# Clustered attention and a SoLU layer: the first batch's clusters in one pass of products, its one-hots on 16 partitions, and a new order of all engines

## The chip, the cores and the metric

One core of a Trainium2 chip. Its engines are TensorE (PE, matmuls; PEld is its weight load), VectorE (DVE), ScalarE (ACT), GpSimd (POOL) and SyncE (SP, which here only issues DMAs). The metric is the device time of one execution in microseconds, as the median of several runs. Engines run at the same time, each in the order in which its instructions were written, and wait for each other through semaphores.

## The reference, cut to what matters

Four batches of eight heads, 768 tokens, 64 columns a head. Each query and each key is assigned to one of 16 clusters of its head (the centroid with the largest normalised product). A query attends only to keys of its own cluster. The result of all heads, 3072 tokens of 512, goes through a layer whose activation is SoLU, with a layer norm behind it.

```python
q_assign = np.argmax(np.einsum('bhsd,hcd->bhsc', q_n, c_n), axis=-1)
k_assign = np.argmax(np.einsum('bhsd,hcd->bhsc', k_n, c_n), axis=-1)
mask = q_assign[:, :, :, None] == k_assign[:, :, None, :]
scores = np.where(mask, scale * np.matmul(q, k.transpose(0, 1, 3, 2)), -1000000000.0)
attn = softmax(scores); x = attn @ v          # B, S, H*D
...
h = x @ w_in                                  # 512 -> 1024
solu = h * softmax(h)
ln = (solu - mu) / np.sqrt(var + 1e-06) * g_ln
out = ln @ w_out                              # 1024 -> 512
```

## The kernel before

**Attention.** The heads go in pairs, 16 of them (batch, pair). Of a pair, q and k are brought to a layout with the head's columns on partitions (`xt`). In the first batch TensorE does this by transposes (`tp`; L396 for the first pair, L403 for the other three) and ScalarE or VectorE copies the result out of PSUM (`xa`, `xb`; L422, L430). In later batches VectorE transposes (`xt`, L444). A cast to bf16 (`ca`, L468 to L472) writes 64 rows of a tile `qk`. Products with the normalised centroids (`cl`, L484 and L489) give a score for each token and cluster; VectorE turns them back (`tb`, L497), takes the largest (`mx`, L510), writes a one-hot (`oh`, L515) and transposes that (`ot`, L521). The one-hots are placed (`pl`, L533 to L540) in `qk` below the 64 rows. So one product of `qk` (`S`, L627) contracts over the 64 columns and over the clusters: a token pair of one cluster gets 1 more. k was scaled by 1/256, and the exponential (`E`, L635) multiplies by 32 and subtracts 32, so a pair of different clusters ends with a factor of exp(-32). No row maximum is subtracted. A head has 16 clusters, and two heads' one-hots come out on 32 partitions; the even head contracts over 80 rows, the odd head over 96, where a memset (`bl`, L549) blanks the 16 rows of the other head in k.

**Three pairs with two tokens in a row.** In the first batch, tokens lie 6 to a partition in DRAM order. Pairs 1 to 3 (`twelve` in the code) load both heads in one DMA and their transposes yield, on the 128 partitions, two neighbouring tokens' columns of one head. So their centroid products, in the kernel before, run in two passes: for each of four groups, one pass for each head, with a table of centroids (`c_by_two`, written by `cf`, L913) that is zero outside the pass's own head; the two add up in PSUM.

**Values and normalisation.** Values (`V`, L654) are products of the exponentials with v and a column of ones; `N` (L666, L679) divides by that column. One PSUM tile holds a group's values, so a group's first value product waits until the group before is normalised.

**SoLU layer.** The 24 units of 128 tokens each take: the transposed x (the first by TensorE, `ptx` L719, and a copy `tx` L725; the others by DMA, L709), eight products with `w_in` (`h`, L744, 128x512 each, two a token of the order), the negated maximum (`hm`, L750), the exponential (`ex`, L756), `u`, the product of the two (L763), the statistics (`bn`, `ag`), a factor (`at`, `al` on GpSimd), u transposed (`tu`, mostly by DMA), eight products with `w_out` (`y`, L813), and the scaling (`sc`, L830 on ScalarE, L832 on VectorE) with the output DMA. The products with `w_in` share three banks of PSUM (`hreg`): the second unit's second half writes a bank that the first unit's `u` reads. `w_out` is centred once (`su` L595 and L598, `me` L604, `ce` L607), its bf16 form is `w_out_c`, whose place holds tables of the first pairs until then. `w_in` is loaded by four DMAs (`li`) and cast by GpSimd (`wi`, L578).

**What sets the order.** Every piece of work is added to a class, `Weave`, with a name (kind and numbers), an engine, what it needs, and an estimated cost. `ORDER` gives for each engine a text of kinds with counts; `AWAY` names the pieces that another engine than the usual one does. `Weave.run` writes the instructions out in this order. The costs serve to interleave the engines' queues at writing; the order within an engine is that of the text. `fl` is two and `wm` 25 `idle` matmuls (L859), which nothing reads.

**The stages.** Until about 45 us there is only attention (loads, transposes, clusters, scores, exponentials, values of the first batch); from the first product with `w_in` at 45.13 us both parts run interleaved; the SoLU layer's last unit ends the kernel.

## Time and profile before

| what | value |
| --- | --- |
| median of 3 runs | 223.9 us (223.2, 223.9, 224.44) |
| span of the profiled execution | 222.4 us |
| TensorE busy | 214.8 us in 2518 instructions |
| VectorE busy | 199.1 us in 363 |
| ScalarE busy | 194.7 us in 382 |
| GpSimd busy | 126.6 us in 252 |
| exponentials of attention, ScalarE | 276, 143.2 us |
| scores, TensorE | 600, 87.4 us |
| values, TensorE | 1152 |
| products with `w_in` (177 of 192 recorded) and `w_out` (169 of 200) | 48.3 and 45.1 us |

The span is that of one profiled execution; the page has no other time for it, so the runs' median, 1.5 us longer, is the time to set it against. A row of groups reads: line, engine, operation, out<-in, partitions x elements, count | busy time, mean of one in ns | idle time of the engine before them and what ended it. A row of the timeline begins with the time in us at which a run of like instructions starts and the time that the run covers. "PEclk" is the TensorE clock that the throttle granted, 1.00 being full. The span is not the sum of anything: an engine's busy time counts only where the others wait for it.

### The profile page before, as it was taken

The numbers are of one execution on the slowest core, as the hardware profiler recorded it, in microseconds if no ns is written. First come the engines' busy times: TensorE is split into PE (matmuls) and PEld (weight loads), VectorE is DVE, ScalarE is ACT, GpSimd is POOL, SyncE is SP. The second block draws the span as 40 slices with busy tenths as digits, with TensorE's granted clock in tenths as the row PEclk, the third lists the DMA queues.
The fourth block names the chain that finished last, engine by engine and source line by source line (L and its number), as shares of the span: only waits on it lengthen the run. The fifth ranks groups of instructions, "written<-read, shape, count | busy, mean of one in ns | idle before, by whom it ended". The sixth has DMA issues, their size and how long they took to land.

```text
span 222.4 us, 6852 instructions
## 1 busy us (share of the span) xinstructions
PE 214.8 (97%) x2518; PEld 151.8 (68%) x2548; DVE 199.1 (90%) x363; ACT 194.7 (88%) x382; POOL 126.6 (57%) x252
## 2 busy tenths in 40 slices
PE   8999899999999999999999999999999999999993
PEld 7765577767777687777777666676767767665452
DVE  2789999999999999899989999999999979999891
ACT  3899999999999999999999989999999989795352
POOL 3189597759884986188837674783746101226131
PEclk9999999999999999999999999999999999999999
DMA  6998989797799979899999897998922928565623
GB/s 157 352 388 221 193 165 284 203 172 165 127 175 237 180 141 215 136 193 166 153 211 239 156 185 150 151 168 158 230 99 50 115 78 145 117 165 121 166 98 143
DMA packets 122433, 38.74 MB, mean 174 GB/s; under 512 B 111448, under 2 KB 117152, under 8 KB 122400
## 3 DMA queue, kind: packets, MB, share of 16 engines
q1 hardware_dynamic: 121680, 37.82, 79.8%
q10 hardware_dynamic: 720, 0.49, 0.7%
q8 instruction: 20, 0.33, 0.7%
q14 instruction: 13, 0.11, 0.1%
HBM read 23.11 MB, written 6.29 MB: 132 GB/s over the span
## 4 chain that ended last, share of the span: by engine, by line
PE 91%; DVE 3%; issue 2%; ACT 2%; DVEq 0%; ACTq 0%
PE sps L627 27%; PE hreg L744 18%; PE yps L813 17%; PE ops L654 16%; PE csc L489 4%; PE hreg L627 2%; PE idle_p L859 2%; PE csc L484 1%; PE hreg L403 1%; PE hreg L396 1%; ACT qk L468 1%; PE hreg L813 1%; ACT e L635 1%; DVE u L763 1%; DVE w_sum L598 1%
## 5 line engine op out<-in xcount | busy, mean ns | idle before, releaser
L635 ACT ACTIVATE e<-sps 128x512 bf16<-128x512 f32 (+1 forms) x276 | 143.2, 609 | 10.2 <-PE sps L627 9.8
L627 PE MATMUL sps<-qk 96*128 96x256 bf16 (+5 forms) x600 | 87.4, 263 | 0.7 <-ACT e L635 0.4
L627 PEld LDWEIGHTS <-qk 96*128 96x128 bf16 (+1 forms) x636 | 59.6, 121 | 24.5 <-issue 8.8
L654 PEld LDWEIGHTS <-e 128*128 128x128 bf16 x1152 | 49.9, 97 | 9.3 <-issue 1.9
L654 PE MATMUL ops<-v,e 128*128 128x65 bf16 x1152 | 54.3, 193 | 0.4 <-DVE x L679 0.4
L744 PE MATMUL hreg<-w_in_sb,xT 128*128 128x512 bf16 x177 | 48.3, 378 | 0.8
L813 PE MATMUL yps<-w_out_c,uT 128*128 128x512 bf16 x169 | 45.1, 379 | 0.8
L540 POOL COPY qk<-oht 32x384 f32<-32x384 f32 (+1 forms) x49 | 24.2, 494 | 21.5 <-DVE oht L521 15.7
L763 DVE TENSOR_TENSOR u<-e_sb,hreg 128x1024 bf16<-128x1024 bf16 (+1 forms) x25 | 29.1, 1169 | 2.7 <-ACT e_sb L756 2.1
L774 DVE BATCH_NORM_STATS2 bs<-u 128x6 f32<-128x512 bf16 x48 | 31.3, 677 | 0.0
L750 DVE TENSOR_REDUCE nmax<-hreg 128x1 f32<-128x1024 f32 x24 | 29.1, 1213 | 2.0 <-PE hreg L744 1.7
L756 ACT ACTIVATE e_sb<-hreg,nmax 128x1024 bf16<-128x1024 f32 x24 | 26.9, 1121 | 4.5 <-DVE nmax L750 4.4
L790 POOL TENSOR_SCALAR esq<-es,mv 128x1 f32<-128x1 f32 x24 | 8.3, 344 | 33.6 <-DVE mv L778 30.3
L813 PEld LDWEIGHTS <-uT 128*128 128x128 bf16 x200 | 18.0, 97 | 13.1 <-issue 0.3
L744 PEld LDWEIGHTS <-xT 128*128 128x128 bf16 x192 | 17.6, 97 | 11.3 <-ACT e L635 0.3
L472 POOL TENSOR_SCALAR qk<-xt 64x768 bf16<-64x768 f32 (+1 forms) x27 | 22.2, 823 | 3.5 <-DVE xt L444 1.7
L444 DVE STREAM_TRANSPOSE xt<-raw 128x768 f32<-128x768 f32 x24 | 22.2, 949 | 0.0
L470 POOL CAST qk<-xt 64x768 bf16<-64x768 f32 (+1 forms) x25 | 20.9, 836 | 1.2
L679 DVE TENSOR_TENSOR x<-ops,den 128x256 bf16<-128x256 f32 (+1 forms) x39 | 18.9, 486 | 1.3
L784 POOL TENSOR_SCALAR es<-esum 128x1 f32<-128x1 f32 x24 | 5.6, 236 | 20.9 <-ACT e_sb L756 20.4
L793 POOL TENSOR_TENSOR alpha<-esq,halves 128x1 f32<-128x1 f32 x24 | 13.8, 574 | 2.0
L830 ACT ACTIVATE y<-yps,alpha 128x512 f32<-128x512 f32 x15 | 10.4, 695 | 4.3 <-PE yps L813 3.0
(85 smaller groups left out, 206.9 us busy)
## 6 DMA issues: line engine op xcount, KB each, us to landing
vf<-in_v_dram SPq DMA_DIRECT2D x16, 384.0 KB, 4.6
out_dram<-y SPq DMA_DIRECT2D x23, 256.0 KB, 2.5
raw<-in_q_dram SPq DMA_DIRECT2D x50, 96.0 KB, 3.8
raw<-in_k_dram SPq DMA_DIRECT2D x50, 96.0 KB, 3.0
w_g<-in_moe_w_out_dram SPq DMA_DIRECT2D x4, 512.0 KB, 8.3
w_st<-in_moe_w_in_dram SPq DMA_DIRECT2D x4, 512.0 KB, 6.2
raw<-in_q_dram SPq DMA_DIRECT2D x3, 384.0 KB, 6.0
raw<-in_k_dram SPq DMA_DIRECT2D x3, 384.0 KB, 7.8
```

Source lines behind the costliest of these rows:

```text
L444: nc.vector.transpose(xt[:], raws[b, p, i][:].rearrange("p j c -> p (j c)"))
L472: VEC[e].tensor_scalar(dst, src, scalar1=inv_C, scalar2=1.0, op0=Alu.mult, op1=Alu.mult)
L540: ins = VEC[e].tensor_copy(dst.bitcast(F32), src.bitcast(F32).unsqueeze(1) .to_broadcast([NB, 2, n // 2]))
L627: ins = nc.tensor.matmul(sps_[n, k][:, c0:c0 + w], side(b, h // 2, 1, h % 2, keys)[r], side(b, h // 2, 0, h % 2, slice(s0 * P, s0 * P + w) ...
L635: ins = nc.scalar.activation(es[n, k][:, :w], sps_[n, k][:, :w], Act.Exp, scale=exp_scale, bias=-exp_scale)
L654: nc.tensor.matmul(opss[g][:, s, :VW], es[n, k][:, c0:c0 + P], v1[slot(b, h // 2)][:, h % 2, kt, :VW], start=(kt == 0), stop=(kt == n_t - 1))
L744: uses(nc.tensor.matmul(hreg[:, at(f, f2)[1], :], xTs[f][:, dc, :], w_in_sb[:, dc, f2 * FF2:(f2 + 1) * FF2], start=(dc == 0), stop=(dc == ...
L750: uses(nc.vector.tensor_reduce(ff[f, "nmax"][:], pair_of(f), axis=AXY, op=Alu.max, negate=True), *both(f))
L756: uses(nc.scalar.activation(ff[f, "e"][:], pair_of(f), Act.Exp, bias=ff[f, "nmax"][:], accum_out=ff[f, "esum"][:]), *both(f))
L763: uses(nc.vector.tensor_tensor(ff[f, "u"][:, r], ff[f, "e"][:, r], pair_of(f)[:, r], op=Alu.mult), *both(f)[r])
L774: nc.vector.bn_stats(ff[f, "bs"][:, f2, :], ff[f, "u"][:, f2, :])
L813: ins = nc.tensor.matmul(dst, ff[f, "uT"][:, at(f, f2)[0] * (n_fc // 2) + c, :], w_out_c[:, fc, cols], start=(fc == fcs[0] and turn == 0 i ...
```

## The change

**One pass for the clusters of pairs 1 to 3 of the first batch.** Each of the four groups gets one product of 384 columns instead of two accumulating ones. Its table, `c_two`, covers both heads at once, so a group's 32 rows hold the two heads' scores for one parity of tokens. The one-hots of such a pair are written 16 columns apart into `apart` (128 x 768, zeroed once at the start), transposed as 128 x 768 into one of two buffers (`turned_apart`), and placed for each head with 16 partitions only, so both heads of these pairs contract over 80 rows and nothing is blanked. `apart` and its transposes lie in the space of `w_out_c`.

```diff
-    def used(hh):
-        return slice(0, D + NC_) if hh == 0 else slice(0, D + 2 * NC_)
+    def used(b, h):
+        return slice(0, D + NC_ * (1 if h % 2 == 0 or twelve(b, h // 2) else 2))
...
-        if twelve(b, p):
-            for c in range(4):
-                i, part = divmod(c, 2)
-                nc.tensor.matmul(csc[c * NB:(c + 1) * NB, :], c_by_two[:, p, 2 * part + hh, :],
-                                 by_two(b, p, i)[:, hh].rearrange("p t n -> p (t n)"),
-                                 start=(hh == 0), stop=(hh == 1), tile_position=(0, c * NB))
-        for c in range(4) if not twelve(b, p) else ():
+        for c in range(4):
             i, part = divmod(c, 2)
...
+            if twelve(b, p):
+                w = c_two[:, p, part, :]
+                x = by_two(b, p, i)[:, part].rearrange("p t n -> p (t n)")
+            else:
+                w, x = c_bd[:, p, :], xts[b, p, i][:, lo + part * n:lo + (part + 1) * n]
+            nc.tensor.matmul(csc[c * NB:(c + 1) * NB, :n], w, x, tile_position=(0, c * NB))
...
+        if twelve(b, p):
+            dst = apart.rearrange("p (u a c) -> p a u c", u=2, c=NB)[:, :, :, :NC_]
+            src, top = (x.rearrange("p (a u) c -> p a u c", u=2)
+                        for x in (by_group(b, p, hf, "cst"), spread_max(b, p, hf)))
...
+        if twelve(b, p):
+            asg[b, p, hf, "oht"] = turned_apart[:, p % 2, :]
+            nc.vector.transpose(turned_apart[:, p % 2, :], apart)
+            return
...
         if twelve(b, p):
-            ins = VEC[e].tensor_copy(
-                every_other(b, p, i, part)[D:D + NB].bitcast(F32),
-                src.bitcast(F32).rearrange("p (t n) -> p t n", t=n_t // 2).unsqueeze(1)
-                .to_broadcast([NB, 2, n_t // 2, P // 2]))
+            dst = (side(b, p, i, part, slice(0, S))[D:D + NC_].bitcast(F32)
+                   .rearrange("p (t u n) -> p u t n", u=2, n=P // 2))
+            src = asg[b, p, hf, "oht"][r.start:r.start + NC_, :].bitcast(F32)
+            ins = VEC[e].tensor_copy(dst, src.rearrange("p (u t n) -> p u t n", u=2, n=P // 2))
```

The dependencies follow: a head's scores need the placed pieces of that head, and the memsets `bl` of these pairs are gone. The first score is written behind all `wm` and `fl`.

**A new order.** All five texts of `ORDER` and the lists of `AWAY` are new, from a search whose model lets SyncE stop at each transfer of instructions. The beginnings of three of the texts, before and after:

```diff
-  SP   ld4 si ld3 lv lg ld3 lo lv lo ld2 lo2 lv ld6 lv ld8 li4 tx
+  SP   ld4 si ld2 lg ld2 lv ld lv lo ld3 lv ld li lo lv ld5 lo2 ld3 li ld li2 ld5 tx
-  PE   fl wm tp2 cp fl4 cl tp2 fl4 cl fl tp S2 cq S tp S tp S2 tp S tp2 S2 cl
+  PE   fl5 wm tp2 fl cp tp fl cl tp fl2 tp cl tp fl S2 cq tp S3 tp S tp S2 tp S tp cl
-  ACT  wa xa2 ca2 xa2 xb ca4 E6 xa E2 xa E xa ca E3 xa3 E4 ca E2 xa E53 ex
+  ACT  wa ca xb2 xa2 ca xa E8 xa E xa2 ca E3 xa3 E8 xa E45 tx E9 ex
```

By `AWAY`, the copy of the first transposed x (`tx0`) goes from VectorE to ScalarE. Both pieces of the last unit's scaling (`sc23.0`, `sc23.1`) are VectorE's, where the first was ScalarE's; of the other 23 scalings ScalarE has 12 (15 before) and VectorE 11 (8 before). The costs given to `add` change with it: the clusters of the three pairs from 1.59 to 0.87, a cast on GpSimd from 0.88 to 0.79, a placing on GpSimd from 0.76 or 0.75 to 0.46, `al` from 1.0 to 0.86.

Three places show what that moves. The first is ScalarE's beginning, up to its first exponentials (`xt` is the transposed q or k in f32, `qk_99` the first pair's bf16 tile, `sps` a bank of scores, `e` an exponential's result). Before:

```order
L422 COPY xt<-hreg 128x2x3x64
L422 COPY xt<-hreg 128x3x64
L468 ACTIVATE qk_99<-xt 64x384 x2
L422 COPY xt<-hreg 128x2x3x64
L422 COPY xt<-hreg 128x3x64
L422 COPY xt<-ops 128x3x64
L468 ACTIVATE qk_99<-xt 64x384 x4
L635 ACTIVATE e<-sps 128x384 x6
```

And after:

```order
L472 ACTIVATE qk_99<-xt 64x384
L426 COPY xt<-ops 128x3x64 x2
L426 COPY xt<-hreg 128x3x64
L434 COPY xt<-hreg 128x384
L472 ACTIVATE qk_99<-xt 64x384
L434 COPY xt<-hreg 128x384
L646 ACTIVATE e<-sps 128x384 x8
```

Of the first pair's six casts two are left on ScalarE, four have gone to VectorE and GpSimd; two copies of the second pair's transposes stand ahead of the first exponential.

The second place is VectorE from its first copy to the first pair's placed one-hots (`cps` holds the transposed centroids, `csc` the cluster scores, `oh` and `oht` the one-hots and their transposes). Before:

```order
L422 COPY xt<-ops 128x3x64
L919 TENSOR_TENSOR c_bd<-cps,own 128x128
L497 STREAM_TRANSPOSE cst<-csc 128x192
L510 TENSOR_REDUCE mx<-cst 128x12
L515 TENSOR_TENSOR oh<-cst,mx 128x192
L521 STREAM_TRANSPOSE oht<-oh 128x192
L540 COPY qk_99<-oht 32x2x96 x2
```

And after:

```order
L426 COPY xt<-hreg 128x2x3x64
L426 COPY xt<-hreg 128x3x64
L474 CAST qk_99<-xt 64x384
L928 TENSOR_TENSOR c_bd<-cps,own 128x128
L426 COPY xt<-hreg 128x2x3x64
L496 STREAM_TRANSPOSE cst<-csc 128x192
L509 TENSOR_REDUCE mx<-cst 128x12
L522 TENSOR_TENSOR oh<-cst,mx 128x192
L531 STREAM_TRANSPOSE oht<-oh 128x192
L551 COPY qk_99<-oht 32x2x96 x3
```

VectorE has three more instructions (two more copies out of PSUM, a cast) ahead of the clusters, and places three pieces of the first half where it placed two.

The third place is where the SoLU layer starts (`xtp` is the first unit's x as TensorE transposed it, `xT` its copy, `nmax` the first unit's maximum). VectorE there before:

```order
L607 SCALAR_TENSOR_TENSOR w_out_c<-w_g,g_ln_115,hreg 128x512
L725 COPY xT<-xtp 128x512
L607 SCALAR_TENSOR_TENSOR w_out_c<-w_g,g_ln_115,hreg 128x512 x3
L666 RECIPROCAL den<-ops 128x4
L679 TENSOR_TENSOR x<-ops,den 128x2x2x64
L607 SCALAR_TENSOR_TENSOR w_out_c<-w_g,g_ln_115,hreg 128x512 x4
L750 TENSOR_REDUCE nmax<-hreg 128x1
```

After, VectorE has no copy of x there, and two of the eight centrings stand behind the maximum:

```order
L618 SCALAR_TENSOR_TENSOR w_out_c<-w_g,g_ln_115,hreg 128x512 x4
L677 RECIPROCAL den<-ops 128x4
L690 TENSOR_TENSOR x<-ops,den 128x2x2x64
L448 STREAM_TRANSPOSE xt<-raw 128x768
L761 TENSOR_REDUCE nmax<-hreg 128x1
L618 SCALAR_TENSOR_TENSOR w_out_c<-w_g,g_ln_115,hreg 128x512 x2
L774 TENSOR_TENSOR u<-e_sb,hreg 128x1024
```

ScalarE has the copy instead, between exponentials of attention:

```order
L646 ACTIVATE e<-sps 128x512 x3
L646 ACTIVATE e<-hreg 128x512
L734 COPY xT<-xtp 128x512
L646 ACTIVATE e<-hreg 128x512
L646 ACTIVATE e<-sps 128x512 x8
L767 ACTIVATE e_sb,esum<-hreg,nmax 128x1024
```

The copy stands behind the 65th exponential; the first unit's own exponential comes 9 exponentials behind it. On TensorE the clusters of the second batch's second pair, ahead of the first product with `w_in` before, stand behind the first eight now.

More of the change, by code (lines that the diff above doesn't have):

```diff
@@ L72 @@
+        tu3 oz
     """
@@ L870 @@
     c_bd = const.tile([P, n_pair, 2 * NC_], F32, name="c_bd")
[L871 to L878 removed]
+    c_two = w_out_c[:, 1, :].bitcast(F32).rearrange("p (a h c) -> p a h c", h=2, c=2 * NC_)
+    apart = w_out_c[:, 2:4, :].rearrange("p a f -> p (a f)")[:, :S]
+    nc.gpsimd.memset(apart.bitcast(F32), 0.0)
+    turned_apart = w_out_c[:, 4:7, :].rearrange("p a f -> p (a f)").rearrange("p (x n) -> p x n", n=S)
     own = const.tile([P, 2 * NC_], F32, name="own")
@@ L925 @@
     add("cq", "PE", 0.28, 0, lambda e: turn_centroids(), ["cn"], ["cp"], take="m")
-    add("cf", "DVE", 0.65, -490, lambda e: keep_by_two(), ["cq"], give="m")
+    add("cf", "DVE", 0.4, -490, lambda e: keep_by_two(), ["cq"], give="m")
     def before(idx, back):
@@ L1005 @@
                     cols = slice(0, S) if hf is None else slice(hf * HALF, (hf + 1) * HALF)
-                    costs = ({"POOL": 0.88, "ACT": 0.76, "DVE": 0.52 + 0.1 * i} if hf is None else
-                             {"POOL": 0.48, "ACT": 0.42, "DVE": 0.33})
+                    costs = ({"POOL": 0.79, "ACT": 0.76, "DVE": 0.52 + 0.1 * i} if hf is None else
+                             {"POOL": 0.45, "ACT": 0.42, "DVE": 0.33})
                     e = "ACT" if hf is not None and i == 1 else "POOL"
@@ L1018 @@
         for hh in range(2):
-            add(f"cv{t}.{hh}", "POOL", 0.455, first - 5,
+            add(f"cv{t}.{hh}", "POOL", 0.45, first - 5,
                 (lambda e, b=b, p=p, hh=hh: cast_v(b, p, hh, e)),
@@ L1032 @@
             old = last[-3] if len(last) >= 3 else None
-            if twelve(b, p):
-                add(f"cl{t}", "PE", 1.59, first - 9,
-                    (lambda e, b=b, p=p, hf=hf: [clusters(b, p, hf, hh) for hh in range(2)]),
-                    kept + ["cf"], take="m")
-            else:
-                add(f"cl{t}", "PE", 0.72 - 0.22 * hf if half else 0.87, first - 9,
-                    (lambda e, b=b, p=p, hf=hf: clusters(b, p, hf)), kept + ["cb"], take="m")
+            add(f"cl{t}", "PE", 0.72 - 0.22 * hf if half else 0.87, first - 9,
+                (lambda e, b=b, p=p, hf=hf: clusters(b, p, hf)),
+                kept + ["cf" if twelve(b, p) else "cb"], take="m")
             add(f"tb{t}", "DVE", 0.37 if half else 0.56, first - 20,
@@ L1049 @@
                 nd += [nm for nm in wv.by if nm.startswith(f"pl{old}.")]
-            add(f"ot{t}", "DVE", 0.33 if half else 0.505, first - 9,
+            add(f"ot{t}", "DVE", 0.33 if half else 0.9 if twelve(b, p) else 0.505, first - 9,
                 (lambda e, b=b, p=p, hf=hf: assign_turn(b, p, hf)), nd)
@@ L1056 @@
                 costs = ({"DVE": 0.3, "POOL": 0.41} if half else
-                         {"POOL": 0.76, "DVE": 0.46} if twelve(b, p) else
-                         {"SP": 0.64, "POOL": 0.75})
+                         {"POOL": 0.46, "DVE": 0.46} if twelve(b, p) else
+                         {"SP": 0.64, "POOL": 0.46})
                 add(f"pl{t}.{i}.{part}", e, costs[e], first - 8 + j * 0.1,
@@ L1062 @@
                     lag=(1.0, 0.7))
-            add(f"bl{t}", "POOL", 0.27, first - 8 + 1.5,
-                (lambda e, b=b, p=p, hf=hf: blank(b, p, hf, e)),
-                [f"pl{t}.1.{part}" for part in range(2)], also={"DVE": 0.2})
+            if not twelve(b, p):
+                add(f"bl{t}", "POOL", 0.37, first - 8 + 1.5,
+                    (lambda e, b=b, p=p, hf=hf: blank(b, p, hf, e)),
+                    [f"pl{t}.1.{part}" for part in range(2)], also={"DVE": 0.2})
     ring_s, ring_e = 3, 9
@@ L1084 @@
                 ts = (f"{b}.{p}",) * 2
-            nd |= {f"pl{ts[1 - x]}.{x}.{part}" for x in range(2) for part in range(2)}
-            nd |= {f"bl{ts[0]}"} if hh else set()
+            nd |= {f"pl{ts[1 - x]}.{x}.{part}" for x in range(2)
+                   for part in ((hh,) if twelve(b, p) else range(2))}
+            nd |= {f"bl{ts[0]}"} if hh and not twelve(b, p) else set()
         nd = sorted(nd)
-        aft = ["S{}.{}".format(*BANKS[i - 1])] if i else []
+        aft = ["S{}.{}".format(*BANKS[i - 1])] if i else [nm for nm in wv.by if re.match("wm|fl", nm)]
         if (n, k) in slots:
```

149 lines of the change are left out of this document (72 added, 77 removed).

## The prediction

> **What bounds the kernel now.** I read the page's busy shares and its chain first, then the busy time of each engine in two stretches, then the rows of time around the three places that the change touches. The page says TensorE, all the way:
>
> ```profile
> PE 214.8 (97%) x2518; PEld 151.8 (68%) x2548; DVE 199.1 (90%) x363; ACT 194.7 (88%) x382; POOL 126.6 (57%) x252
> PE 91%; DVE 3%; issue 2%; ACT 2%; DVEq 0%; ACTq 0%
> q8 instruction: 20, 0.33, 0.7%
> ```
>
> A page's share is a mean over stages. The busy times by stretch (the columns are named in the first row) split it:
>
> ```profile
> core 0: us, PE busy (x) PEld busy (x) DVE busy (x) ACT busy (x) POOL busy (x), PEclk, DMA share, GB/s
> 10.60:47.30 36.70, 35.52 (x458) 24.90 (x458) 34.52 (x68) 35.83 (x79) 29.35 (x50) 1.00 0.92 242
> 45.10:219.00 173.90, 171.82 (x1915) 120.14 (x1941) 161.19 (x278) 154.51 (x295) 96.31 (x185) 1.00 0.80 157
> ```
>
> In the opening, 10.6 to 47.3 us, ScalarE is busy 35.83 of 36.7 us: nothing but exponentials, and copies and casts between them. VectorE has 34.52. TensorE shows 35.52, but a matmul's end is modelled and overlaps the next one's start, so this isn't 35.5 us of issue. From 45.1 to 219.0 us TensorE is the fullest by 10 us, and there it is the bound. So **two limits follow each other**: ScalarE (VectorE close by) until the MoE's first product with `w_in`, TensorE from there to the end. ScalarE's rows in the opening:
>
> ```profile
> 8.68 2.02 ACT L468 ACTIVATE qk<-xt 64x384 bf16<-64x384 f32 x4
> 10.61 2.34 ACT L635 ACTIVATE e<-sps 128x384 bf16<-128x384 f32 x6
> 19.83 0.86 ACT L468 ACTIVATE qk<-xt 64x768 bf16<-64x768 f32 x1
> 23.40 1.25 ACT L635 ACTIVATE e<-sps 128x384 bf16<-128x384 f32 x3 [0.36 <-PE sps L627]
> 44.20 1.26 ACT L635 ACTIVATE e<-hreg 128x512 bf16<-128x512 f32 x2
> ```
>
> The first exponential starts at 10.61, when ScalarE's own casts (8.68 to 10.70) let it; 44.20 is the 65th. Between them this view shows one idle of weight, 0.36 us at 23.40.
>
> **The change, part by part.** *The clusters.* The three pairs' products go from two passes to one:
>
> ```profile
> 13.61 1.50 PE L484 MATMUL csc<-xt,w_out_c 128*32 128x384 f32 x16
> 42.24 0.85 PE L489 MATMUL csc<-xt,c_bd 128*32 128x384 f32 x8
> ```
>
> 16 records took 1.50 us; the new form has the tile shapes and the count of the second row, 0.85. That is 0.65 us a pair, 1.95 in all, **and all of it lies in the opening**, which ScalarE sets: the exponentials there stand in one queue, and TensorE's free time cannot shorten it. I cost it at nothing by itself; if the opening were TensorE's, it would be worth the whole 1.95. The other side effects of the new form:
>
> ```profile
> L627 PE MATMUL sps<-qk 80*128 80x256 bf16 x216 | 35.9, 275 | 0.6 <-ACT e L635 0.4
> L627 PE MATMUL sps<-qk 96*128 96x256 bf16 x216 | 35.5, 274 | 0.0
> L521 DVE STREAM_TRANSPOSE oht<-oh 128x384 bf16<-128x384 bf16 x15 | 8.5, 565 | 0.1
> L444 DVE STREAM_TRANSPOSE xt<-raw 128x768 f32<-128x768 f32 x24 | 22.2, 949 | 0.0
> L533 POOL COPY qk<-oht 32x384 f32<-32x384 f32 x12 | 7.9, 662 | 2.9 <-DMA raw<-in_q_dram 2.3
> L549 POOL MEMSET qk<- 16x384 f32 x10 | 4.1, 412 | 0.4
> ```
>
> Scores over 80 rows instead of 96 cost the same (275 and 274 ns). The transpose of one-hots grows from 384 to 768 bf16 columns; no row has it, the nearest are 565 ns (half the columns) and 949 (768 columns of f32): 0.57 to 0.95 each, I take 0.95, so 3 x 0.38 = 1.2 us more on VectorE. The 12 copies that place them (662 ns on GpSimd) shrink to 16 partitions, between the memset's 412 and 662; two of the 12 go to VectorE. Three memsets go (3 x 0.4). GpSimd has room for either end.
>
> *The start.* Ahead of the first transposes `idle` now runs 35 times instead of 27 (`fl5 wm` for `fl wm`), and the first exponential's own road changes:
>
> ```profile
> 0.97 3.06 PE L859 MATMUL idle_p<-w_out_c 128*128 128x128 bf16 x27 [0.97 <-DVE halves L863]
> 3.96 1.01 PE L396 MATMUL hreg<-ident_f,raw 64*64 64x64 f32 x25
> 5.72 1.06 PE L859 MATMUL idle_p<-w_out_c 128*128 128x128 bf16 x8
> 8.10 0.62 PE L859 MATMUL idle_p<-w_out_c 128*128 128x128 bf16 x8
> 9.90 0.48 PE L627 MATMUL sps<-qk 80*128 80x384 bf16 x2
> 7.38 0.38 DVE L497 STREAM_TRANSPOSE cst<-csc 128x192 f32<-128x192 f32 x1 [1.13 <-PE csc L489]
> 8.58 0.38 DVE L521 STREAM_TRANSPOSE oht<-oh 128x192 bf16<-128x192 bf16 x1
> 8.99 0.57 DVE L540 COPY qk<-oht 32x192 f32<-32x192 f32 x2
> ```
>
> One early `idle` matmul costs (3.06 - 1.06) / 19 = 0.105 us, so eight are 0.85, and the transposes, released at 3.96 now, start near 4.8. Everything up to the one-hots hangs on them, so I shift the row at 7.38 by the same 0.85 (the eight `idle` matmuls that now stand at 5.72 become two, but in their place come a transpose and, on ScalarE, a cast ahead of a copy that the clusters need). VectorE then places three pieces instead of two before the first score: another 0.57 / 2 = 0.28. First score: now 9.90, which left 0.34 us after the two copies' end (9.56) for GpSimd's; then 7.38 + 0.85 + (9.56 - 7.38) + 0.28 = 10.7, with the start of the product 10.75. First exponential about 0.4 later, 11.15, since ScalarE no longer has casts in front (six half casts there become two): **+0.5** against 10.61. Bounds: 0 (the start's slack takes it) to +0.8.
>
> [...] Eight `idle` matmuls took 1.06 us at 5.72 and 0.62 at 8.10, though the first ten microseconds show a granted clock of 1.00 throughout:
>
> ```profile
> 0.00:10.00 10.00, 9.03 (x162) 7.46 (x163) 4.61 (x20) 5.32 (x12) 2.99 (x20) 1.00 0.77 237
> ```
>
> So the granted clock's column doesn't show this rate. [...]
>
> *ScalarE's queue to the first `w_in` product.* One whole cast leaves it (0.86 by the row at 19.83), and the 0.36 us of idle at 23.40 goes, since TensorE now has 1.95 us less in front of those scores: **-1.2**. Late next there is VectorE's placing of pair 1's one-hots, which I put 0.3 to 0.5 us ahead of the scores that need it. Against this, the copy of the first transposed x moves to ScalarE and stands behind the 65th exponential:
>
> ```profile
> 44.75 0.54 PE L654 MATMUL ops<-v,e 128*128 128x65 bf16 x12
> 45.13 1.89 PE L744 MATMUL hreg<-w_in_sb,xT 128*128 128x512 bf16 x7
> 50.13 0.38 PE L627 MATMUL sps<-qk 80*128 80x256 bf16 x2 [0.40 <-ACT e L635]
> 51.17 0.38 PE L744 MATMUL hreg<-w_in_sb,xT 128*128 128x512 bf16 x1
> 51.39 0.60 PE L627 MATMUL sps<-qk 96*128 96x256 bf16 x4
> 47.13 1.23 DVE L750 TENSOR_REDUCE nmax<-hreg 128x1 f32<-128x1024 f32 x1
> 49.63 1.22 DVE L763 TENSOR_TENSOR u<-e_sb,hreg 128x1024 bf16<-128x1024 bf16 x1 [0.20 <-ACT e_sb L756]
> L607 DVE SCALAR_TENSOR_TENSOR w_out_c<-w_g,g_ln,hreg 128x512 bf16<-128x512 f32 x8 | 5.5, 740 | 0.0
> L740 ACT COPY uT<-utp 128x512 bf16<-128x512 bf16 x1 | 0.6, 577 | 0.0
> ```
>
> The 65th would start at 44.20 + 0.5 - 1.2 = 43.5; half a row of two, about 0.5 (1.26 less the overlap and tail of the last), it holds the queue, then the copy takes 0.58 (L740 has its shape on ScalarE): the first `w_in` product comes at 44.6 instead of 45.13. By the queue alone it would have been -0.7, so the copy's wait gives back **+0.2** (0 to +0.5). What queues behind the copy is the next exponential. The product's weights can't be what is late: SyncE issues the four loads of `w_in` further ahead in the new order, and their casts on GpSimd move ahead with them.
>
> *TensorE from there.* Before, the clusters at 42.24 (0.85, of which the next row hides a little: 0.8) were done ahead of the first `w_in` product; now those of that pair stand behind it: **+0.8** of TensorE's own time, in the stage that it bounds. Beyond, both orders hold the same matmuls. TensorE's waits in the old order's first six microseconds of this stage: from 45.13 to 51.17 it issues 12 products with `w_in` (0.216 each, seven from 45.13 in 1.89 with the last one's 0.38), 14 scores (0.11 each: four in 0.60, two in 0.38) and 36 of values (0.032: twelve in 0.54, the last of 0.19), which is 2.6 + 1.5 + 1.2 = 5.3 of the 6.0 us; the rest, 0.4 of it shown at 50.13, are waits for exponentials. With ScalarE ahead I let these go: **-0.7**. Late next is VectorE: the product at 51.17, the third of the second unit's four, writes a bank that the first unit's `u` (49.63 to 50.85) reads. In the new order 6.7 us of matmuls stand between the first product and that one, so TensorE is there at 51.3. When is `u`?
>
> *VectorE up to there.* To its first `nmax` the queue gains 1.2 (transposes), 0.9 (three half places), 0.8 (two of the 16-partition copies), 1.1 (three casts of halves, estimated at 0.36 each from the 0.86 of a whole one less a fixed part), 0.6 (one more normalisation), loses 1.5 (two of the eight centrings, 0.74 each, which go behind it) and about 1.4 (two value casts, a cast, the copy of x, a smaller centroid table): +1.7, of which some 1.4 (copies and a cast) stand ahead of the row at 7.38, where VectorE waits today (1.13 there alone). With the start's 0.85 that is +1.1, and its wait for the clusters of pair 1,
>
> ```profile
> 15.17 0.58 DVE L497 STREAM_TRANSPOSE cst<-csc 128x384 f32<-128x384 f32 x1 [0.71 <-PE csc L484]
> ```
>
> has that much to give back: 0.71 goes. So `nmax` and `u` come 0.4 later, `u` ends at 51.3, and TensorE, there at 51.3 too, loses about **+0.3** to the handing over and to chance (0 to +1.5).
>
> *The end.* The last two scalings ran beside each other; now both are VectorE's:
>
> ```profile
> 218.79 0.53 ACT L830 ACTIVATE w_in_sb<-hreg,alpha 128x320 f32<-128x320 f32 x1 [0.87 <-PE hreg L813]
> 219.13 0.42 DVE L832 TENSOR_SCALAR w_in_sb<-hreg,alpha 128x192 f32<-128x192 f32 x1 [1.40 <-PE hreg L813]
> ```
>
> One after the other they take 0.53 + 0.42 = 0.95 from 218.79 on, where 0.76 did (to 219.55); the piece that goes out last is the small one: **+0.1**.
>
> *SyncE's stops.* The 20 transfers of instructions are there, but SyncE has no share in the chain: what its stops delay lands early enough now, so planning for them gains nothing that this trace shows. If new places bring a load late, that is a wait in the term above.
>
> Sum against the span of 222.4: +0.5 - 1.2 + 0.2 + 0.8 - 0.7 + 0.3 + 0.1 = 0.0, a span of 222.4. The median of the runs is 223.9, 1.5 us over the span (the ends around it, and the runs' spread); I leave these 1.5 as they are: **223.9**, no change: the 1.95 us are taken from an engine that waits, and what ScalarE's queue gains is spent by a later start and by clusters that move behind it.
>
> **The rivals.** *TensorE bounds the opening too.* For it: 97% busy, 91% of the chain, and the chain runs through the rows at 13.61 and 42.24. Against it: the exponentials follow each other with 0.36 us of idle. If it holds, the first score isn't what matters and the 1.95 us come off whole: 223.9 - 1.95 = 221.9.
>
> *VectorE takes over.* The half second by which I let it arrive late rests on its waits giving way. They may not: between 10.6 and 47.3 it is busy 34.5 of 36.7 us, and if the 0.71 stays and the new copies cost their upper rows (0.66 for 0.42, twice), `u` of the first unit ends 1.1 + 0.5 later, at 52.4. It decides from the point where that is later than TensorE's arrival at the second unit's third product, 51.3: TensorE then stands 1.1 us there instead of 0.3, and the same again at the next unit, since VectorE has no idle time to catch up in. That is 223.9 + 0.8 + 0.8 = 225.5, slower.
>
> [...]
>
> That the order does nothing for SyncE is no rival with a time of its own: it is what the forecast assumes.
>
> **How the numbers follow.** About 0.5%, 1.1 us, is what a measurement of this kernel can tell from no change: 222.8 to 225.0. The forecast has 0.39 and the early clock 0.05; both lie within. TensorE all the way has 0.32, faster. VectorE late has 0.24, slower. So faster 0.32, same 0.44, slower 0.24. Both signs hold weight, so the forecast's own range, 222.8 to 225.0, holds the start's 0 to +0.8 and the copy's 0 to +0.5; new waits of up to +1.5 go beyond it. The range with the rivals reaches from 221.6 (the 1.95 with a start that isn't late) to 225.5.
>
> **What would show it.** Right: first exponential at 11.0 to 11.3; ScalarE without idle from there to the 65th, at 43.3 to 43.8; first `w_in` product at 44.4 to 44.9; TensorE's busy time up to there some 2 us lower than before, as idle. Wrong: a first exponential before 10.6 (the fillers cost nothing), a first `w_in` product before 43.7 (TensorE set the opening: 221.9), or TensorE standing a microsecond before the second unit's third `w_in` product (the slow case).

## The result, and the profile after

| kernel | median, us | ratio to before | runs |
| --- | --- | --- | --- |
| before | 223.98 | | 4 |
| the change | 231.74 | 1.0352 [1.0323, 1.0381] | 4 (231.25 to 232.35) |

The change is slower by 3.5%, outside the range. In the experiments below, single runs far off (234.49 us of e5_n, 274.26 of e9_n2, 227.96 of e11_su, 316.21 and 228.38 of before) are left out of the ratios. The profiled execution of it has a span of 230.3 us against 222.4, so 7.9 us are to be found. The page of the changed kernel (busy shares; the chain by engine; the granted clock in 40 slices of 5.8 us):

```profile
PE 219.2 (95%) x2524; PEld 152.3 (66%) x2524; DVE 205.0 (89%) x362; ACT 195.3 (85%) x378; POOL 129.1 (56%) x250
PEclk9999985999999999999999999999999999999999
PE 73%; POOL 7%; DVE 6%; DMA 4%; SPq 3%; issue 3%; ACT 2%; DVEq 0%; POOLq 0%; ACTq 0%
```

Two things are new. TensorE has 73% of the chain instead of 91%, and GpSimd, VectorE, DMAs and SyncE's queue have parts of it. And the granted clock has a hole: slices 6 and 7 are below full. The busy times by stretch (columns as in the prediction: TensorE, its weight loads, VectorE, ScalarE, GpSimd, granted clock) put it exactly; the changed kernel:

```profile
10.00:20.00 10.00, 8.55 (x95) 5.97 (x93) 8.79 (x20) 8.92 (x23) 7.74 (x14) 1.00 1.01 293
20.00:30.00 10.00, 9.15 (x117) 6.25 (x113) 9.70 (x19) 9.78 (x23) 6.42 (x10) 1.00 0.88 243
30.00:40.00 10.00, 8.62 (x88) 5.64 (x86) 7.89 (x14) 7.09 (x14) 9.38 (x16) 0.66 0.90 242
32.00:33.00 1.00, 0.71 (x5) 0.56 (x5) 1.00 (x2) 0.61 (x2) 0.94 (x2) 0.81 0.44 57
33.00:34.00 1.00, 1.00 (x16) 0.91 (x14) 0.68 (x1) 1.00 (x3) 0.92 (x2) 0.50 0.13 21
38.00:39.00 1.00, 1.00 (x9) 0.08 (x2) 0.96 (x2) 0.25 (x1) 0.94 (x2) 0.50 0.89 319
39.00:40.00 1.00, 1.00 (x12) 0.81 (x13) 1.00 (x2) 0.37 (x1) 1.00 (x2) 0.77 1.15 284
```

And the kernel before in the last of these stretches:

```profile
30.00:40.00 10.00, 9.79 (x149) 7.47 (x147) 9.46 (x18) 10.00 (x22) 8.13 (x18) 1.00 0.96 247
```

From 32.6 to 39.5 us the clock stands at half. ScalarE, which was busy for all of 30 to 40 us before, is busy for 7.09 of 10, and VectorE for 7.89: both wait for a slow TensorE. What came ahead of it shows in TensorE's row of time (in brackets: idle time, and who ended it):

```profile
29.54 0.82 PE L638 MATMUL sps<-qk 80*128 80x256 bf16 x6
31.01 0.55 PE L665 MATMUL ops<-v,e 128*128 128x65 bf16 x12 [0.65 <-DVE x L690]
32.29 0.72 PE L638 MATMUL hreg<-qk 80*128 80x256 bf16 x4 [0.73 <-POOL qk L544]
37.48 1.51 PE L490 MATMUL csc<-xt,c_bd 128*32 128x384 f32 x8
```

Two waits of 0.65 and 0.73 us, for a normalisation of VectorE and for a one-hot that GpSimd places, and then the clock is halved: eight cluster products take 1.51 us where they took 0.85. GpSimd's row of time shows why its piece came late:

```profile
26.35 1.50 POOL L544 COPY qk<-w_out_c 16x384 f32<-16x384 f32 x2 [2.73 <-DVE w_out_c L528]
27.91 0.50 POOL L569 CAST v<-vf 128x384 bf16<-128x384 f32 x1
28.48 0.50 POOL L544 COPY qk<-w_out_c 16x384 f32<-16x384 f32 x1
29.04 0.81 POOL L589 CAST w_in_sb<-w_st 128x512 bf16<-128x512 f32 x1
29.83 1.26 POOL L476 TENSOR_SCALAR qk<-xt 64x768 bf16<-64x768 f32 x1
31.18 0.49 POOL L569 CAST v<-vf 128x384 bf16<-128x384 f32 x1
31.74 1.41 POOL L544 COPY qk<-w_out_c 16x384 f32<-16x384 f32 x2
```

It stood 2.73 us for VectorE's transpose of pair 2's one-hots, placed three pieces, and had a cast of `w_in` (0.81), one of k (1.26) and two of v in its order before the fourth, which the scores of pair 2's second head need.

The first product with `w_in` then comes at 49.09 instead of 45.13 us: 4.0 of the 7.9 us arise ahead of it, 3.9 behind it.

### The profile page after: what moved, and what is told of

The parts are those of the page before. It is cut to its first block, busy times and chain, and to the rows that moved or that the text cites. A ratio compares the mean times of both kernels' runs of the same rounds, so it can differ in the third digit from the quotient of the medians.

```text
span 230.3 us, 6830 instructions
## 1 busy us (share of the span) xinstructions
PE 219.2 (95%) x2524; PEld 152.3 (66%) x2524; DVE 205.0 (89%) x362; ACT 195.3 (85%) x378; POOL 129.1 (56%) x250
## 4 chain that ended last, share of the span: by engine, by line
PE 73%; POOL 7%; DVE 6%; DMA 4%; SPq 3%; issue 3%; ACT 2%; DVEq 0%; POOLq 0%; ACTq 0%
PE sps L638 20%; PE hreg L755 16%; PE yps L824 16%; PE ops L665 12%; PE csc L490 4%; SPq L440 3%; DMA uT<-u 2%; DMA raw<-in_q_dram 2%; PE idle_p L870 2%; POOL qk L544 2%; ACT e L646 1%; PE hreg L638 1%; POOL qk L474 1%; POOL qk L476 1%; POOL qk L551 1%
## 5 line engine op out<-in xcount | busy, mean ns | idle before, releaser
L638 PE MATMUL sps<-qk 80*128 80x256 bf16 (+5 forms) x600 | 94.7, 266 | 1.3 <-POOL v L1297 0.5
L638 PEld LDWEIGHTS <-qk 80*128 80x128 bf16 (+1 forms) x636 | 61.1, 122 | 32.1 <-issue 9.2
L665 PEld LDWEIGHTS <-e 128*128 128x128 bf16 x1152 | 53.9, 99 | 13.9 <-DVE x L690 3.3
L665 PE MATMUL ops<-v,e 128*128 128x65 bf16 x1152 | 59.2, 195 | 2.0 <-DVE x L690 2.0
L755 PE MATMUL hreg<-w_in_sb,xT 128*128 128x512 bf16 x192 | 53.5, 379 | 0.5 <-ACT xT L734 0.5
L824 PE MATMUL yps<-w_out_c,uT 128*128 128x512 bf16 x184 | 51.1, 378 | 0.2 <-DMA uT<-u 0.2
L474 POOL CAST qk<-xt 64x768 bf16<-64x768 f32 (+1 forms) x27 | 22.2, 823 | 7.3 <-DVE xt L426 4.0
L755 PEld LDWEIGHTS <-xT 128*128 128x128 bf16 x192 | 16.6, 97 | 10.0 <-ACT xT L734 0.8
L569 POOL CAST v<-vf 128x384 bf16<-128x384 f32 x28 | 15.1, 541 | 2.5 <-DMA vf<-in_v_dram 1.4
```

The lines of the kernel that those rows point to most:

```text
L474: VEC[e].tensor_copy(dst, src)
L638: ins = nc.tensor.matmul(sps_[n, k][:, c0:c0 + w], side(b, h // 2, 1, h % 2, keys)[r], side(b, h // 2, 0, h % 2, slice(s0 * P, s0 * P + w) ...
L665: nc.tensor.matmul(opss[g][:, s, :VW], es[n, k][:, c0:c0 + P], v1[slot(b, h // 2)][:, h % 2, kt, :VW], start=(kt == 0), stop=(kt == n_t - 1))
L755: uses(nc.tensor.matmul(hreg[:, at(f, f2)[1], :], xTs[f][:, dc, :], w_in_sb[:, dc, f2 * FF2:(f2 + 1) * FF2], start=(dc == 0), stop=(dc == ...
L824: ins = nc.tensor.matmul(dst, ff[f, "uT"][:, at(f, f2)[0] * (n_fc // 2) + c, :], w_out_c[:, fc, cols], start=(fc == fcs[0] and turn == 0 i ...
```

## Experiments

Two theories for the first part: **A**, the waits empty TensorE, the clock falls, and that is the loss; **B**, VectorE and GpSimd set this stretch anyway and the low clock only fills their time. Two for the change as a whole: **C**, the order alone; **D**, the new form of the clusters too.

**e1_fill** repeats work in the two waits.

```diff
-        for h, kt, s0, w, c0 in u["banks"][k]:
+        done["S"] += 1
+        for h, kt, s0, w, c0 in u["banks"][k] * (4 if done["S"] == 39 else 1):
...
-        for kt in range(n_t):
+        done["V"] += 1
+        for kt in [*range(n_t)] * (5 if done["V"] == 18 else 1):
```

> The changed kernel, with the matmuls ahead of TensorE's two waits near 31 us issued again (one bank of scores four times instead of once, one block of values five times): 1.4 us of work that nobody needs, laid into 1.7 us in which TensorE waits. Theory A (the low granted clock is the loss: the waits empty TensorE, the clock then falls to half for some 7 us, and that costs half of it): the granted clock stays at 1.00 from 30 to 40 us, the first product with w_in comes near 46 instead of 49.1, and the run takes 228.0 to 229.0 us. Theory B (VectorE and GpSimd set this stretch anyway, the low clock only fills their time): the clock may hold, but the run stays at 231 to 232.5.

Measured: 229.13 us, ratio 1.0228 [1.0199, 1.0258], first product with `w_in` at 46.94. The granted clock is 1.00 throughout in the profiled run, and its mean is 0.997 to 1.00 in the four, as in those of before. Work that nobody needs makes the kernel 2.6 us faster. Theory A holds; the time lies 0.1 us above its range.

**e2_place** takes the second wait's cause away.

```diff
-        pl2 cv pl wi ca sg cv pl2 ca z pl ca     (POOL, from pair 2's pieces on)
+        pl4 cv wi ca sg cv pl ca z pl ca
```

> The changed kernel with one edit of order: GpSimd places the last piece of pair 2's one-hots directly behind the other three, ahead of two casts of v, a cast of w_in and a cast of k. That takes away the cause of the second wait (0.73 us at 32.3). Theory A: with one wait of the two gone the clock holds, and the run takes 227.5 to 228.5 us; if 0.65 us of waiting is enough to drop it, 231. Theory B: at most the 0.7 us, 231.

Measured: 229.16 us, 1.0234 [1.0217, 1.0251], clock 1.00. TensorE's row of time in e2_place:

```profile
30.61 0.55 PE L665 MATMUL ops<-v,e 128*128 128x65 bf16 x12 [0.51 <-DVE x L690]
31.00 0.60 PE L638 MATMUL hreg<-qk 80*128 80x256 bf16 x4
33.97 0.92 PE L665 MATMUL ops<-v,e 128*128 128x65 bf16 x24 [0.42 <-DVE x L690]
46.31 0.88 PE L755 MATMUL hreg<-w_in_sb,xT 128*128 128x512 bf16 x3 [0.59 <-ACT xT L734]
```

The first wait is still there, the second gone, and the clock holds; the first product with `w_in` comes 2.8 us earlier than in the change. One place in GpSimd's order cost a third of the loss. The gain was 0.7 to 1.7 us more in the expectation than on the chip.

**e3_alg** has the new form in the order of before (three memsets left out, which it doesn't need).

> The new one-pass clusters, spaced one-hots and 16-partition placing in the order of before (all five texts and the list of moved pieces are those of before, only three memsets that are no longer needed are left out). Theory C (the loss is the new order's, the new form costs nothing in an opening that ScalarE sets): 223.0 to 224.5 us. Theory D (the new form's longer transposes and one-hots make VectorE and GpSimd late whatever the order): 226 to 231. If TensorE bound the opening as well, 222.0.

Measured: 224.98 us, 1.0068 [1.0027, 1.011], five runs. Three of them had the full clock and took 224.17 to 224.98, two had a mean of 0.992 and took 226.18 and 226.57. The median is 0.5 us above the range of theory C, that of the three runs at full clock (224.52) at its edge. Theory C is right for the bulk: nearly all of the 7.8 us are the order's. But 1.95 us of TensorE's time went and nothing came of it, with a little loss. Where it went, from 30 us on, VectorE and then TensorE in e3_alg:

```profile
29.52 1.21 DVE L518 TENSOR_TENSOR w_out_c<-cst,mx 128x384 bf16<-128x384 f32 x1
30.65 0.98 DVE L605 SCALAR_TENSOR_TENSOR w_sum<-w_g,g_ln,w_sum 128x512 f32<-128x512 f32 x1
31.56 0.96 DVE L524 STREAM_TRANSPOSE w_out_c<-w_out_c 128x768 bf16<-128x768 bf16 x1
32.62 0.42 DVE L686 TENSOR_TENSOR x<-ops,den 128x256 bf16<-128x256 f32 x1
```

```profile
33.20 0.35 PE L661 MATMUL ops<-v,e 128*128 128x65 bf16 x6 [1.37 <-POOL qk L540]
```

The view names GpSimd's copy, which ended last. But a value product needs the one PSUM tile that the normalisation at 32.62 empties; that ends at 33.04, and ahead of it, in VectorE's order, stand a one-hot of 1.21 us, a sum and the 768-column transpose. Before, this normalisation came at 31.70.

**e4_sc7** puts one scaling back on ScalarE. VectorE in the changed kernel near 134 us:

```profile
134.39 0.75 DVE L843 TENSOR_SCALAR y<-yps,alpha 128x512 f32<-128x512 f32 x1 [1.29 <-POOL alpha L804]
135.05 0.97 DVE L448 STREAM_TRANSPOSE xt<-raw 128x768 f32<-128x768 f32 x1
136.73 0.56 DVE L690 TENSOR_TENSOR x<-ops,den 128x384 bf16<-128x384 f32 x1
```

> The changed kernel with one scaling (of unit 7, near 134 us) on ScalarE again instead of VectorE, where it waits 1.3 us for GpSimd's factor and holds up VectorE's queue. If such waits of VectorE are where the later part of the loss is made: 0.7 us less, 231.0. If the late loads of q and k are what counts there, 231.7 as before.

Measured: 229.96 us, 1.0255 [1.0215, 1.0295]; TensorE's wait there is gone. The number is no measure of it: the fall of the clock was shorter in its runs (means of 0.990 to 0.999, 3.41 us in the profiled one against 6.83).

**e5_n** tests where e3_alg lost: one move on VectorE.

```diff
-        cv ot su N su2 tb mx N oh su ot N xt2
+        cv ot su N su2 tb mx N oh N ot su xt2
```

> The new form of the clusters in the order of before (as e3_alg), with one move on VectorE: the fourth normalisation, for which TensorE stood 1.4 us at 33.2 us, goes ahead of a sum of w_out's rows and the 768-column transpose of pair 3's one-hots. Theory D2 (the new form's 1.95 us on TensorE are real, and e3_alg gives them back because the longer one-hots and transposes on VectorE push the normalisations, behind which the values wait): that wait goes, the run gains 0.7 to 1.4 us on e3_alg, 223.6 to 224.3, level with the kernel before or below it. Theory S (ScalarE's queue of exponentials sets the opening, as the prediction had it): TensorE's wait goes and nothing comes of it, 225.0.

Measured: 224.11 us, 1.0026 [1.001, 1.0042]. By the medians that is 0.9 us less than e3_alg, as theory D2 had it. But the two intervals overlap, and e3_alg's median has two runs with a fallen clock in it: at full clock e3_alg's median is 224.52, 0.4 above e5_n, and the first product with `w_in` comes at 45.08 instead of 45.34. So this run doesn't decide between D2 and S. What it shows is that the wait was for the normalisation: TensorE's products that stood at 33.20 start at 31.59, and VectorE is waited for again at 33.88:

```profile
31.59 0.35 PE L661 MATMUL ops<-v,e 128*128 128x65 bf16 x6
33.88 1.70 PE L486 MATMUL csc<-xt,c_bd 128*32 128x384 f32 x8 [0.34 <-DVE xt L444]
```

**e6_x** has e2_place with the copy of x on VectorE and the scalings of units 7 and 10 on ScalarE.

```diff
-  ACT  E45 tx E9 ex ... E12 sc ex E16 ex E8 sc ... ex E6 ca E2 ex
+  ACT  E54 ex       ... E12 sc ex E7 sc E9 ex E8 sc ... ex E6 ca sc E2 ex
-  DVE  xt ce2 N ce4
+  DVE  xt ce2 N tx ce4     (and two sc left out further on)
```

> e2_place with three pieces moved between ScalarE and VectorE: the copy of the first transposed x back to VectorE, and the scalings of units 7 and 10 (where VectorE had made TensorE wait 0.7 us each, at 133 and 160 us) to ScalarE. If such waits add up on TensorE: 0.6 (the copy) + 0.7 + 0.7 less than e2_place, 227.1. If TensorE then stands for something else (the late loads of q and k): 228.5 or more.

Measured: 228.54 us, 1.0209 [1.018, 1.0238]: 0.6 less than e2_place by the medians, where 2.0 was expected, with intervals that overlap; the profiled execution (228.43) shows 1.2 less span than that of e2_place, and the waits at all three places gone. From its first product with `w_in` (46.17) to its end are 179.7 us, against 180.8 in e2_place, 181.2 in the change and 177.3 before.

**e7_fl** starts e2_place with 27 idle matmuls instead of 35 (`fl wm` for `fl5 wm`).

> e2_place with fl wm at the start instead of fl5 wm: 27 idle matmuls ahead of the first transposes instead of 35, as before the change. The prediction's term for the start says +0.5 us for the eight, so: first exponential 0.5 earlier and 228.7. If the opening is set by VectorE and GpSimd further on: first exponential earlier, first product with w_in where it was, 229.1. If the eight keep the clock up: a later first exponential.

Measured: 229.40 us, 1.0259 [1.0221, 1.0297]; first exponential at 10.80 instead of 10.89. Four runs from 228.21 to 230.79 can't show half a microsecond. The start of TensorE's row in e7_fl, then in the change, then the transposes in e1_fill, which begins exactly as the change does:

```profile
0.97 3.06 PE L870 MATMUL idle_p<-w_out_c 128*128 128x128 bf16 x27 [0.97 <-DVE halves L874]
3.96 1.01 PE L400 MATMUL hreg<-ident_f,raw 64*64 64x64 f32 x25
```

```profile
0.97 3.92 PE L870 MATMUL idle_p<-w_out_c 128*128 128x128 bf16 x35 [0.97 <-DVE halves L874]
4.82 0.83 PE L400 MATMUL hreg<-ident_f,raw 64*64 64x64 f32 x25
```

```profile
4.82 1.01 PE L400 MATMUL hreg<-ident_f,raw 64*64 64x64 f32 x25
```

The same 25 transposes behind the same 35 idle matmuls take 0.83 us in one trace and 1.01 in the other, so it isn't the longer stretch of idle matmuls that makes them faster. TensorE's rate rises at another moment in each run. The same goes for the 27: the eight idle matmuls that took 1.06 us at 5.72 in the kernel before take 0.61 in e3_alg, which begins in the same order:

```profile
5.52 0.61 PE L866 MATMUL idle_p<-w_out_c 128*128 128x128 bf16 x8
```

The record of the clock in each trace begins where the rate rises (ahead of that moment an idle matmul takes 313 or 314 ns in the mean in the traces of before and of the change, behind it 220 to 224): at 6.90 us in the trace of before, 6.72 in e7_fl, 6.59 in e1_fill, 6.50 in e6_x, 5.32 in the change, 5.19 in e3_alg, 5.13 in e2_place. Only traces with a like rise can be compared. e7_fl has its first exponential at 10.80, e1_fill and e6_x at 11.27 and 11.26: the eight idle matmuls cost that exponential 0.5 us, as the prediction's term had it. Against e2_place the early rise hides it.

**e8_nfirst** turns VectorE's order of e2_place between 20 and 32 us, normalisations first.

```diff
-  DVE  ot N ca su tb mx pl2 xa oh ot su N tb mx oh su N ot su xt N
+  DVE  ot N pl2 ca su tb mx xa oh ot N su tb mx oh N ot su2 xt N
```

> e2_place with VectorE's order turned in one place, between 20 and 32 us: two pieces of pair 1's one-hots are placed, and two normalisations done, as soon as what they need is there, and a copy and the sums of w_out's rows follow them. TensorE's waits at 23 (1.1), 27 (0.4) and 30 us (0.7) should go. If waits for VectorE set the rest of the opening's loss: first product with w_in 1.0 to 2.0 us earlier than in e2_place (44.3 to 45.3), run 227.2 to 228.2. If ScalarE's queue is the limit: 0.5 earlier at most, 228.7 to 229.2.

A miss: 231.24 us, 1.0338 [1.0312, 1.0364], and the clock fell again, at 35.74 us. The two sums that now stand behind the transpose made the next normalisation late (35.10 instead of 33.40), and TensorE waited 1.58 us for that one. The fall explains little of this miss: one of the four runs has a mean clock of 0.999 and took 230.95 us, in the midst of the others. But it gives the fall a second place, and so a comparison. TensorE's busy time (second number in a row, after the length) in the 3.41 us ahead of a fall, in the change and in e8_nfirst:

```profile
29.22:32.63 3.41, 2.03 (x38) 1.56 (x35) 3.38 (x6) 3.16 (x7) 3.29 (x6) 1.00 1.06 272
```

```profile
32.33:35.74 3.41, 1.78 (x26) 1.15 (x25) 3.34 (x6) 3.27 (x7) 3.14 (x6) 1.00 0.77 179
```

Both falls come a whole number of 3.41 us behind the rise: 8 from 5.32 to 32.63 (27.31 us), 9 from 5.03 to 35.74 (30.71 us). The same goes for a2 (8 from 4.92 to 32.23) and e4_sc7 (8 from 4.87 to 32.18), and the falls last one such length (3.41 us, e4_sc7 and e8_nfirst) or two (6.83 us, the change and a2). So in these four traces the clock's changes in the opening lie on steps of 3.41 us, whose start differs from run to run (4.87 to 5.32 us), and the stretches to compare are those between two steps. Of the ten profiled kernels whose clock did not fall on the way, the emptiest such stretches (up to 210 us) are these of e2_place and e3_alg:

```profile
22.20:25.61 3.41, 2.37 (x39) 1.81 (x37) 3.28 (x6) 2.78 (x8) 1.42 (x3) 1.00 1.14 295
```

```profile
29.08:32.49 3.41, 2.45 (x36) 1.66 (x35) 3.38 (x6) 3.41 (x8) 3.16 (x5) 1.00 0.88 144
```

The clock fell behind 1.78 (e8_nfirst), 2.01 (a2, e4_sc7) and 2.03 us (the change) of 3.41, and not behind 2.37 and more. e3_alg has 3.41 us that are as empty, but they lie across two steps:

```profile
29.80:33.21 3.41, 2.04 (x35) 1.55 (x34) 3.38 (x6) 3.41 (x9) 3.01 (x7) 1.00 0.86 133
```

That would explain why two of its five runs fell and three did not, by where the steps lay; those two were not profiled, so it is not shown.

**e9_n2, e10_xt, e11_su** go on from e5_n: the first normalisation ahead of a sum; two transposes of the next batch ahead of a sum; the last two sums together. The **a2** run is the change once more, beside the first two.

```diff
-  DVE  xa gk su2 N tb mx xa oh cv ot su N su2 tb        (e5_n)
+  DVE  xa gk su N tb mx xa oh cv ot su2 N su2 tb        (e9_n2)
-  DVE  oh N ot su xt2 N su tb mx su oh N                (e9_n2)
+  DVE  oh N ot xt2 su N su tb mx su oh N                (e10_xt)
+  DVE  oh N ot xt2 su N su2 tb mx oh N                  (e11_su)
```

> e5_n with the first normalisation on VectorE moved too: it goes ahead of a sum of w_out's rows (1.2 us), and with it the copy at 22.7 us for which TensorE stood 0.6. If TensorE's waits for VectorE are what eats the 1.95 us: TensorE's waits at 21 and 23 us (0.7 and 0.6) go, first product with w_in at 44.3 to 44.8 instead of 45.1, run 223.2 to 223.8, level with the kernel before or just below. If ScalarE's queue holds: first product with w_in at 45.0 and 224.1, as e5_n.

> e9_n2 with two transposes of the next batch's q and k ahead of the last sum of w_out's rows on VectorE, since the cluster products at 34 us waited for them. By the same theory: another 0.3 to 0.6 us, 222.8 to 223.4, below the kernel before. If the exponentials then wait for pair 3's placed one-hots all the same: as e9_n2.

> e10_xt with the last two sums of w_out's rows done one after the other on VectorE, ahead of a transpose and a maximum of the next batch's clusters; in e10_xt TensorE stood 0.6 us at 37.9 for the last sum. If VectorE still has slack somewhere in the opening: that wait goes too and the run takes 223.3 to 223.7, below the kernel before. If VectorE is simply full there (each thing brought forward makes another late): another wait takes its place and the run takes 223.8 to 224.4, level.

> The changed kernel once more, beside the two others on the same chip. If the clock's fall near 31 us is a property of this order: every run again with a mean granted clock of 0.985 to 0.995 and 231.0 to 232.5 us; a run at 1.00 would be near 229.

Measured: e9_n2 223.88 us, 0.9998 [0.9983, 1.0012]; e10_xt 224.34, 1.0017 [1.0005, 1.0029]; e11_su 224.35, 1.0017 [1.0004, 1.003]. e9_n2 is level with the kernel before, and its first product with `w_in`, at 44.95, lies nearer to what was said for ScalarE's queue (45.0) than to 44.3 to 44.8. e10_xt, expected to be faster, is not; e11_su came as its second theory had it. In e9_n2 the 41st exponential starts at 31.00, 1.5 us earlier than before (32.52); 0.55 of this is the first exponential's (10.06, as in e3_alg with its rise at 5.19, instead of 10.61 with one at 6.90). Then TensorE waits for VectorE's transposes, and ScalarE for TensorE (e9_n2, one row of each):

```profile
33.75 1.70 PE L486 MATMUL csc<-xt,c_bd 128*32 128x384 f32 x8 [0.73 <-DVE xt L444]
35.87 1.08 ACT L642 ACTIVATE e<-sps 128x512 bf16<-128x512 f32 x2 [1.21 <-PE sps L634]
```

In e11_su TensorE's wait for the last sum is gone, and another has come behind it (e11_su, TensorE's row of time):

```profile
38.72 0.35 PE L661 MATMUL ops<-v,e 128*128 128x65 bf16 x6 [0.73 <-DVE x L686]
```

From the first exponential to the 31st e9_n2 needs 16.2 us (before: 16.8), from there to the 65th 17.8 (before: 16.8). In these runs each piece that VectorE does earlier makes another late. No version here beats the kernel before.

a2: 231.37 us, 1.0321 [1.0279, 1.0362]. Its four runs sort by the clock: 229.69 at a mean of 1.00, 230.76 at 0.991, 231.97 and 232.56 at 0.985. The expectation had every run with a fall; one had none, and took what was said for it.

## Why the prediction was wrong, step by step

*The new form, costed at nothing: right, for a reason that was only half right.* The 1.95 us lie in the opening and are worth nothing there (e3_alg 1.0068, e5_n 1.0026, e9_n2 0.9998). The prediction gave ScalarE's queue as the cover. The traces of e3_alg, e5_n, e9_n2 and e11_su show VectorE taking the time back: what moves on VectorE brings forward comes late again behind it, and TensorE's wait goes from one normalisation or transpose of VectorE's to the next. How much of the 1.95 us VectorE eats is not measured: moves on VectorE alone are worth 0.4 us with the clock at full (e3_alg to e5_n) and 0.2 more (e9_n2), near the noise.

*VectorE's added work: the transposes were sized right, the one-hots grew too.* By groups, the changed kernel:

```profile
L528 DVE STREAM_TRANSPOSE w_out_c<-w_out_c 128x768 bf16<-128x768 bf16 x3 | 2.9, 976 | 0.1
L522 DVE TENSOR_TENSOR w_out_c<-cst,mx 128x384 bf16<-128x384 f32 x3 | 2.1, 711 | 0.0
L522 DVE TENSOR_TENSOR oh<-cst,mx 128x384 bf16<-128x384 f32 x12 | 6.5, 541 | 0.1
L544 POOL COPY qk<-w_out_c 16x384 f32<-16x384 f32 x10 | 5.9, 587 | 3.7 <-DVE w_out_c L528 2.7 <-DVE den L677 0.5
```

976 ns was taken as 0.95. The one-hots that are written apart cost 711 against 541 in the mean, three times 0.17, which the prediction had not. The form alone isn't the reason: the three took 0.93, 0.55 and 0.66 us, so one was no longer than the dense ones; what made the others longer is open. The copies of 16 partitions cost 587, inside the bounds of 412 and 662.

*The start, +0.5: somewhat too small.* The first exponential came at 10.98 (11.15 was said, from 10.61), but the rate rose at 6.90 us in the trace of before and at 5.32 in that of the change. Of traces with a like rise, e6_x and e1_fill, which begin as the change does, have 11.26 and 11.27 against 10.61; with a rise at 5.03, e8_nfirst has 10.85 against 10.06 in e3_alg (5.19), which begins in the order of before. So the start costs 0.65 to 0.8, at the upper end of the bounds given, and 0.5 of it are the eight idle matmuls (e7_fl). For the early clock, which the prediction gave 0.05, no run shows that the longer stretch of idle matmuls brings it: the rate rose at 4.87 to 6.59 us in the traces with 35 of them and at 4.61 to 6.90 in those with 27. It did rise earlier in the profiled run of the change than in that of before.

*ScalarE's queue to the 65th exponential, -1.2: this is the step that failed.* It was to start at 43.5; it started at 47.77. The prediction asked once what is late next, named VectorE's placing of pair 1's one-hots, put it 0.3 to 0.5 us ahead, and went on with ScalarE as the bound. Up to the 31st exponential that does little (27.63 against 27.44). At pair 2 VectorE and GpSimd are late one after the other: the two waits of 0.65 and 0.73 us, both in one stretch of 3.41 us, and the clock. From the first exponential to the 65th, 32.4 us were forecast (43.5 less 11.15), against 33.6 before; the change takes 36.8, and e2_place, where the clock holds, 33.9. So 2.9 of the 4.4 us are the clock's, and 1.5 are the step itself: even at full clock ScalarE's queue does not get shorter, since it goes on waiting for scores that wait for VectorE and GpSimd (in e2_place TensorE stands 0.93 us at 24.01 for a one-hot that VectorE places). Of the whole run, e1_fill and e2_place take 2.6 us off by keeping the clock; a2's runs with and without the fall differ by 1.1 to 2.9. Of the fall the prediction had nothing, though it had TensorE's two rates at the start (1.06 and 0.62 us for eight idle matmuls). That TensorE waits in the opening ("TensorE's free time cannot shorten it") was taken as harmless, and it wasn't in the change, with TensorE busy for 2.03 of 3.41 us ahead of the fall.

*The copy of x on ScalarE, +0.2 (0 to +0.5).* TensorE waited 0.5 to 0.6 for it (e2_place's last row above); in e6_x, where VectorE copies, that wait is gone. Right in sign, too small. With the clock held and without this wait, the first product with `w_in` still comes 1.0 us later than before (46.17, e6_x), of which the start is the larger part by the figures above; no run tried the rest.

*Behind the first `w_in` product: +0.4 was said (clusters +0.8, waits -0.7, `u` +0.3), 3.9 came.* The place that was named, `u` of the first unit and the second unit's products, shows no wait of TensorE in the change. What it waits for there, from the view of waits from 49.2 us on (us in all, times, longest):

```profile
PE ops L665 <- DVE x L690: 1.1, 2, 0.6
PE sps L638 <- POOL qk L560: 0.4, 1, 0.4
```

Normalisations again: VectorE does three more scalings of 0.75 us, and one of them stood 1.29 us for GpSimd's factor ahead of a normalisation. The prediction counted the moved scalings only at the end of the kernel. e6_x takes both waits away, with the copy's: 0.6 us by the medians, 1.2 by the spans, of which 1.1 lie behind the first product. With it, 2.4 us remain there; 0.8 of them would be the clusters that were moved there, by the prediction's figure, which no run tried alone. The last 1.6 us are not settled: a memset of GpSimd's (0.4, in the view above) and SyncE's queue and loads of q, which have 3% and 2% of the chain now, are candidates. The prediction left the loads out of its sum, and no run tried them.

*The rival "VectorE takes over"* named the right engine, 20 us too late, and put 1.6 us on it where the change lost 7.8.

*The tail, +0.1: right.* The two scalings take 0.88 us together, where they took 0.76 (the change, VectorE's row of time):

```profile
226.31 0.88 DVE L843 TENSOR_SCALAR w_in_sb<-hreg,alpha 128x320 f32<-128x320 f32 x2 [0.58 <-PE hreg L824]
```
